# Softmax row sums from chunks added on Pool and split in two fp16 halves, in a fused attention and SwiGLU kernel

## Chip, cores, metric

One core of one Trainium2 chip. The metric is device microseconds of one execution; a quoted time is the median of three to seven executions, with the lowest and highest in brackets. "Clock" is the mean TensorE clock that the profile says was granted, as a share of full speed. Engines are named as in the profile: PE is TensorE, ACT is ScalarE, DVE is VectorE, POOL is GpSimd. SBUF and PSUM are the two kinds of memory that the kernel takes its tiles from: its matmuls write to tiles in PSUM (the pools with `space=PSUM`), and all other tiles lie in SBUF.

## The reference

Attention over 8 batches x 12 heads of 448 tokens with head size 64, then a gated feed-forward layer (FFN) over all 3584 tokens:

```python
scores = (q @ k.T) / sqrt(64);  attn = softmax(scores);  o = attn @ v     # per head
x = o.transpose(0, 2, 1, 3).reshape(3584, 768)
g = x @ w_gate                                  # 768 -> 1536
out = (g * sigmoid(g) * (x @ w_val)) @ w_out    # 1536 -> 768
```

Inputs and output are fp32. The kernel computes in fp16 with fp32 accumulation.

## The kernel before

Heads are worked in 48 *pairs*; two pairs (an even `p` and `p + 1`) make a *quad*, whose four heads go to four 32-column tiles of TensorE (form `112*32` in the profile; sixteen such matmuls of 0.355 us each, four a tile, take 0.76 us together). The program is one loop over pairs. A pass is called a *slot*; it computes the scores and exp of its own pair in two halves, and in between the row sums and PV (attn times v) of an earlier quad, and pieces of the FFN (gate `gp`, value `vp` and output `op` steps). The FFN pieces fill TensorE, so that it hardly has to wait for exp (2.2 us in all in the profile before).

`E[pr]` holds exp of the scores of a pair, transposed: keys on partitions, in 4 chunks of 112, and for each of the two heads 448 queries. The sum over keys is a matmul with a matrix of ones, 4 chunks x 4 heads = 16 matmuls a quad:

```python
def sums(p0):
    acc = ps_f.tile([128, 512], FP32, tag="f")
    for c in range(NC):                       # 4 chunks
        for j in range(4):                    # 4 heads of the quad
            nc.tensor.matmul(
                acc[ts(j, 32), 0:S], lhsT=ones[:],
                rhs=E[p0 + j // 2][:, c, j % 2, :],
                start=(c == 0), stop=(c == NC - 1),
            )
    ...
```

The loop, cut to what the change touches. Pool's queue takes, in this order: the copies of `prep` (order q and k for the transposing transfer), the loads of q and k, and in every third slot a load of v:

```python
for pr in range(END):
    ...
    qk_half(pr, 0)                              # scores, exp, chunks 0 and 1
    prep(pr + 3)                                # Pool: two copies
    if not odd: load_qk16(pr + LA)              # Pool issues two loads
    if (pr + 2) % GP == GP - 1: load_v(...)     # Pool issues a load of v
    if not odd: deferred.extend(recips(pr - 2, sums(pr - 2)))
    work = odd and pr > FIRST + 1
    if work: scaled(pr - 3, 0, pv(pr - 3, 0))   # PV, first half of the quad
    carry = ffn_run(...)                        # FFN steps; DVE's deferred work in between
    qk_half(pr, 1)                              # chunks 2 and 3
    if work: scaled(pr - 3, 1, pv(pr - 3, 1))   # PV, second half
    carry = ffn_run(...)
```

Each engine runs its own queue in program order (in slot 31 of the changed kernel, shown below, Pool's adds stand behind a load that waits 2.98 us). [...] The rest of the kernel is unchanged but for a scratch tile.

The softmax here doesn't subtract the row's maximum and nothing guards it: scores larger than these inputs give would overflow.

## Time and profile before

| | before |
|---|---|
| time, us (three executions; with a fourth, 463.63) | 463.38 (462.26 to 464.27) |
| span of the profiled execution, us | 460.2 |
| TensorE busy / idle in that span, us | 452.3 / 7.9 |
| TensorE clock | 1.00 |
| Pool busy, us | 104.2 |

Idle is span minus busy. TensorE is all but always at work, and 7.9 us of idle time is mostly the start and the end of the run. For such a kernel there is one question to a change: what does it take from TensorE's work, and what does it add to TensorE's waits?

### The profile page before, as it was taken

The numbers are of one execution on the slowest core, as the hardware profiler recorded it, in microseconds if no ns is written. First come the engines' busy times: TensorE is split into PE (matmuls) and PEld (weight loads), VectorE is DVE, ScalarE is ACT, GpSimd is POOL, SyncE is SP. The second block draws the span as 40 slices with busy tenths as digits, with TensorE's granted clock in tenths as the row PEclk, the third lists the DMA queues.
The fourth block names the chain that finished last, engine by engine and source line by source line (L and its number), as shares of the span: only waits on it lengthen the run. The fifth ranks groups of instructions, "written<-read, shape, count | busy, mean of one in ns | idle before, by whom it ended". The sixth has DMA issues, their size and how long they took to land.

```text
span 460.2 us, 14133 instructions
## 1 busy us (share of the span) xinstructions
PE 452.3 (98%) x6367; PEld 227.8 (49%) x6367; DVE 236.8 (51%) x371; ACT 243.0 (53%) x353; POOL 104.2 (23%) x164
## 2 busy tenths in 40 slices
PE   8899999999999999999999999999999999999996
PEld 3344444444455555444455555544445556554454
DVE  2765663666764554564654554636555546334310
ACT  7986666656664555454646555455555562222222
POOL 8455606334150132303123040210200000000000
PEclk9999999999999999999999999999999999999999
DMA  9999999995793484662758393903603111100123
GB/s 133 195 200 201 192 180 183 223 154 80 90 113 57 78 126 49 114 102 31 118 58 119 67 131 74 142 6 76 98 10 56 37 37 36 36 11 25 36 68 103
DMA packets 82045, 44.23 MB, mean 96 GB/s; under 512 B 36673, under 2 KB 78529, under 8 KB 81985
## 3 DMA queue, kind: packets, MB, share of 16 engines
q0 software_dynamic: 42368, 23.37, 39.2%
q1 hardware_dynamic: 39520, 19.92, 23.8%
q8 instruction: 49, 0.80, 0.7%
q14 instruction: 12, 0.09, 0.1%
q10 hardware_dynamic: 96, 0.05, 0.0%
HBM read 47.19 MB, written 11.01 MB: 126 GB/s over the span
## 4 chain that ended last, share of the span: by engine, by line
PE 95%; ACT 3%; DMA 1%; DVE 0%; issue 0%; SPq 0%; ACTq 0%
PE gp L264 15%; PE op L261 14%; PE vp L264 13%; PE vp L261 11%; PE op L264 10%; PE s L196 10%; PE gp L261 9%; PE acc L212 9%; PE acc L234 4%; ACT E L203 2%; DMA rk<-in_k_dram 1%; PE tp L184 1%; PE wp L103 0%; PE tp L167 0%; DVE qkT L175 0%
## 5 line engine op out<-in xcount | busy, mean ns | idle before, releaser
L203 ACT ACTIVATE E<-s 112x896 f16<-112x896 f32 x192 | 164.6, 917 | 24.3 <-PE s L196 24.1
L280 ACT ACTIVATE sg<-gp 128x384 f32<-128x384 f32 (+1 forms) x96 | 52.3, 545 | 85.4 <-PE gp L264 54.7
L292 DVE SCALAR_TENSOR_TENSOR t<-sg,gp 128x384 f32<-128x384 f32 (+1 forms) x96 | 58.5, 610 | 64.3 <-ACT sg L280 64.2
L325 ACT ACTIVATE osb<-op 128x384 f32<-128x384 f32 (+1 forms) x57 | 27.7, 486 | 100.5 <-PE op L261 56.3
L264 PE MATMUL gp<-X,wg 128*32 128x512 f16 (+1 forms) x1416 | 78.1, 355 | 0.0
L249 DVE RECIPROCAL R<-ssb 128x112 f32<-128x112 f32 x92 | 73.1, 827 | 0.7
L295 DVE SCALAR_TENSOR_TENSOR hts<-t,vp 128x384 f16<-128x384 f32 (+1 forms) x96 | 59.6, 621 | 23.3 <-PE vp L264 7.9
L261 PE MATMUL op<-wo,hts 128*128 128x384 f16 (+1 forms) x408 | 68.6, 322 | 0.0
L264 PE MATMUL vp<-X,wv 128*32 128x512 f16 (+1 forms) x1224 | 66.9, 353 | 0.0
L226 DVE TENSOR_TENSOR X<-acc,R 128x448 f16<-128x448 f32 x48 | 29.7, 624 | 64.9 <-PE acc L212 63.1
L261 PE MATMUL vp<-X,wv 128*128 128x384 f16 (+1 forms) x270 | 58.4, 352 | 0.0
L196 PE MATMUL s<-qkT 64*128 64x448 f16 x384 | 54.8, 355 | 2.5 <-ACT E L203 2.2
L261 PEld LDWEIGHTS <-hts 128*128 128x128 f16 x408 | 38.9, 98 | 28.2 <-issue 3.0
L264 PEld LDWEIGHTS <-wg 128*32 128x32 f16 x1416 | 37.8, 97 | 29.6
L264 PE MATMUL op<-wo,hts 128*32 128x384 f16 x1104 | 48.9, 326 | 0.0
L261 PE MATMUL gp<-X,wg 128*128 128x384 f16 (+1 forms) x222 | 47.4, 350 | 0.0
L264 PEld LDWEIGHTS <-wv 128*32 128x32 f16 x1224 | 32.7, 97 | 25.5
L212 PE MATMUL acc<-E,vt 112*32 112x448 f16 x768 | 45.2, 355 | 0.0
L126 POOL DMA_DIRECT2D vt<-in_v_dram x16 | 12.3, 772 | 142.7 <-PE acc L212 141.7
L261 PEld LDWEIGHTS <-wv 128*128 128x128 f16 x270 | 25.3, 98 | 26.9 <-issue 4.8
L264 PEld LDWEIGHTS <-hts 128*32 128x32 f16 x1104 | 29.5, 97 | 16.3
L154 POOL COPY qk<-q 112x512 f16<-112x512 f16 x37 | 22.9, 620 | 63.9 <-DMA qkT<-qk 46.4
(38 smaller groups left out, 201.2 us busy)
## 6 DMA issues: line engine op xcount, KB each, us to landing
vt<-in_v_dram POOLq DMA_DIRECT2D x16, 336.0 KB, 5.2
q<-in_q_dram POOLq DMA_DIRECT2D x22, 224.0 KB, 5.9
k<-in_k_dram POOLq DMA_DIRECT2D x22, 224.0 KB, 6.7
out_dram<-osb SPq DMA_DIRECT2D x7, 336.0 KB, 3.1
wg<-in_moe_w_gate_dram POOLq DMA_DIRECT2D x8, 288.0 KB, 11.1
wv<-in_moe_w_val_dram POOLq DMA_DIRECT2D x8, 288.0 KB, 11.4
wo<-in_moe_w_out_dram POOLq DMA_DIRECT2D x2, 1152.0 KB, 21.6
out_dram<-osb SPq DMA_DIRECT2D x8, 288.0 KB, 2.9
```

Of the source, the lines that this page charges most:

```text
L154: nc.gpsimd.tensor_copy(dst, src)
L196: nc.tensor.matmul(s[:, hx, 0:S], lhsT=t[ts(hx, 64)].rearrange("p c q -> p (c q)")[:, c * P : c * P + 128], rhs=t[ts(hx, 64), NC:, :].rear ...
L203: nc.scalar.activation(E[pr][:, c], s[0:P, :, 0:S], AF.Exp, scale=sm_scale)
L212: nc.tensor.matmul(acc[ts(j, 32), 0:S], lhsT=v16[g][:, 2 * r + j % 2, c, :].rearrange("p (d t) -> p t d", t=2)[:, t], rhs=E[p0 + j // 2][: ...
L226: nc.vector.tensor_tensor(X[kk][:, hp + t, ts(bb, S)], acc[:, 0:S], R[p0][:], ALU.mult)
L249: lambda i=i: nc.vector.reciprocal(rt[:, ts(i, P)], ssb[:, ts(i, P)]) for i in range(4)
L261: nc.tensor.matmul(dst, lhsT=lhsT, rhs=rhs, start=start, stop=stop)
L264: nc.tensor.matmul(dst[ts(j, 32), :], lhsT=lhsT[:, ts(j, 32)], rhs=rhs, start=start, stop=stop)
L280: nc.scalar.activation(sg[:, 0:n], gp[:, 0:n], AF.Tanh, scale=0.5)
L292: nc.vector.scalar_tensor_tensor(t1[:, 0:n], sg[:, 0:n], 1.0, gp[:, 0:n], ALU.add, ALU.mult)
L295: nc.vector.scalar_tensor_tensor(hts[:, fb, 0:n], t1[:, 0:n], 0.5 * HS, vp[:, 0:n], ALU.mult, ALU.mult)
L325: nc.scalar.activation(osb[:, ds(m0, w)], op[:, 0:w], AF.Copy, scale=1.0 / HS)
```

## The change

The intent: move part of the row sums from the bound engine to idle ones. For every other quad from pair 12 on (quads starting at 12, 16, 20 ... 40, eight in all), Pool adds the four chunks of E in fp32. So that TensorE can sum the result over partitions in fp16 without losing its precision, ACT rounds a quarter of the sum to fp16 (the high half) and DVE computes the rest (the low half); TensorE then needs 2 x 4 matmuls with a matrix of fours in place of 4 x 4. To give Pool time, from quad 12 on every quad's row sum and PV come one slot later: the sum in slot p + 3, PV in slot p + 4. So the quad that starts at 28 has its sum in slot 31.

```diff
+    def presummed(pr):
+        return PS <= pr < NPAIR - 4 and pr // 2 % 2 == 0          # PS = 12
+    def presum_a(pr):
+        ts_ = [attp.tile([P, S], FP32, tag="tsum", bufs=3, name="tsum") for _ in range(2)]
+        tsum[pr] = ts_
+        for hx in range(2):
+            nc.gpsimd.tensor_tensor(ts_[hx][:], E[pr][:, 0, hx], E[pr][:, 1, hx], ALU.add)
+    def presum_b(pr):
+        for hx in range(2):
+            t = tsum[pr][hx]
+            for c in (2, 3):
+                nc.gpsimd.tensor_tensor(t[:], t[:], E[pr][:, c, hx], ALU.add)
+    def presum_hi(pr):
+        hl[pr] = attp.tile([P, 2, 2, S], FP16, tag="hl", bufs=2, name="hl")
+        for hx in range(2):
+            nc.scalar.activation(hl[pr][:, 0, hx], tsum[pr][hx][:], AF.Copy, scale=0.25)
+    def presum_lo(pr, hx):
+        nc.vector.scalar_tensor_tensor(
+            hl[pr][:, 1, hx], tsum[pr][hx][:], 0.25, hl[pr][:, 0, hx], ALU.mult, ALU.subtract)
     def sums(p0):
-        for c in range(NC):
+        pre = presummed(p0)
+        n = 2 if pre else NC
+        for c in range(n):
             ...
-                    lhsT=ones[:],
-                    rhs=E[p0 + j // 2][:, c, j % 2, :],
+                    lhsT=ones[:, int(pre)],                       # ones or fours
+                    rhs=src[:, c, j % 2, :],                      # src: hl or E
 [... in the loop ...]
-            elif not odd and pr >= 2:
+            elif not odd and 2 <= pr < PS + 2:
                 deferred.extend(recips(pr - 2, sums(pr - 2)))
+            elif odd and pr >= PS + 3 and pr - 3 < NPAIR:
+                pop_deferred(99)
+                deferred.extend(recips(pr - 3, sums(pr - 3)))
+            if presummed(pr - 1):
+                presum_b(pr - 1)
 [... PV of quad pr - 3 or, from slot 16 on, of quad pr - 4; FFN; second half of scores; PV ...]
+            if presummed(pr):
+                presum_a(pr)
+            if presummed(pr - 1):
+                presum_hi(pr - 1)
+                for hx in range(2):
+                    deferred.append(lambda p=pr - 1, hx=hx: presum_lo(p, hx))
```

Cut from the diff: for room, the raw q and k tiles have four buffers in place of five (`RB`) and small pairs share them, and DVE's `t1` is written into `sg`. What is left of DVE's deferred work (reciprocals, low halves) is now all issued ahead of PV.

More of the change, by code (lines that the diff above doesn't have):

```diff
@@ L21 @@
 LA = 6
-RB = 5
+RB = 4
+PS = 12
 FIRST = 6
@@ L77 @@
     ps_f = ctx.enter_context(tc.tile_pool(name="ps_f", bufs=3, space=PSUM))
-    ones = consts.tile([P, 32], FP16, name="ones")
-    warm = consts.tile([128, 512], FP16, name="warm")
+    ones = consts.tile([P, 2, 32], FP16, name="ones")
+    warm = ep.tile([128, 512], FP16, tag="E", name="warm")
     ident = consts.tile([P, P], FP16, name="ident")
@@ L93 @@
     raw = {}
+    pairbuf = []
+    tsum = {}
+    hl = {}
     v16 = {}
@@ L112, in load_qk16 @@
     def load_qk16(pr, n=2):
-        q16 = raws.tile([P, 4, NC, D], FP16, tag="rq", bufs=RB, name="q16")
-        k16 = raws.tile([P, 4, NC, D], FP16, tag="rk", bufs=RB, name="k16")
-        for dst, src in ((q16, q), (k16, k)):
+        h0 = 2 if pr == 2 else 0
+        if h0 == 0:
+            pairbuf.clear()
+            for tag in ("rq", "rk"):
+                pairbuf.append(raws.tile([P, 4, NC, D], FP16, tag=tag, bufs=RB, name=tag))
+        for dst, src in zip(pairbuf, (q, k)):
             flat = src.rearrange("b h s d -> (b h) s d")[2 * pr : 2 * pr + 2 * n]
-            nc.gpsimd.dma_start(dst[:, 0 : 2 * n], flat.rearrange("h (p c) d -> p h (c d)", c=NC))
+            nc.gpsimd.dma_start(
+                dst[:, h0 : h0 + 2 * n], flat.rearrange("h (p c) d -> p h (c d)", c=NC)
+            )
         for i in range(n):
-            raw[pr + i] = (q16[:, 2 * i : 2 * i + 2], k16[:, 2 * i : 2 * i + 2])
+            raw[pr + i] = tuple(x[:, h0 + 2 * i : h0 + 2 * i + 2] for x in pairbuf)
     def load_v(g, lo=0, hi=2 * GP):
@@ L228, in scaled @@
         )
+    def presummed(pr):
[16 more added lines that the diff above has]
+        nc.vector.scalar_tensor_tensor(
+            hl[pr][:, 1, hx], tsum[pr][hx][:], 0.25, hl[pr][:, 0, hx], ALU.mult, ALU.subtract
+        )
     def sums(p0):
         acc = ps_f.tile([128, 512], FP32, tag="f")
-        for c in range(NC):
+        pre = presummed(p0)
+        n = 2 if pre else NC
+        for c in range(n):
             for j in range(4):
+                src = hl[p0 + j // 2] if pre else E[p0 + j // 2]
                 nc.tensor.matmul(
                     acc[ts(j, 32), 0:S],
-                    lhsT=ones[:],
-                    rhs=E[p0 + j // 2][:, c, j % 2, :],
+                    lhsT=ones[:, int(pre)],
+                    rhs=src[:, c, j % 2, :],
                     start=(c == 0),
-                    stop=(c == NC - 1),
+                    stop=(c == n - 1),
                 )
@@ L290, in ffn1_steps @@
                 )
-            t1 = fp.tile([128, 512], FP32, tag="t1")
             nc.vector.scalar_tensor_tensor(
-                t1[:, 0:n], sg[:, 0:n], 1.0, gp[:, 0:n], ALU.add, ALU.mult
+                sg[:, 0:n], sg[:, 0:n], 1.0, gp[:, 0:n], ALU.add, ALU.mult
             )
             nc.vector.scalar_tensor_tensor(
-                hts[:, fb, 0:n], t1[:, 0:n], 0.5 * HS, vp[:, 0:n], ALU.mult, ALU.mult
+                hts[:, fb, 0:n], sg[:, 0:n], 0.5 * HS, vp[:, 0:n], ALU.mult, ALU.mult
             )
@@ L354 @@
         nc.vector.memset(warm[:], 0.0)
-        nc.vector.memset(ones[:], 1.0)
+        nc.vector.memset(ones[:, 0], 1.0)
+        nc.vector.memset(ones[:, 1], 4.0)
         load_qk16(1, 1)
@@ L428 @@
         carry = 0.0
-        DELAY = 2
-        END = NPAIR + 2
+        END = NPAIR + 3
         add_at = {FIRST: 0}
         for i in range(1, B - 1):
-            add_at[NHP * (i + 1) + DELAY] = i
+            add_at[NHP * (i + 1) + (2 if NHP * i + 4 < PS else 3)] = i
         for pr in range(END):
@@ L470 @@
                     scaled(pr - 3, t, halves[t])
-            work = odd and pr > FIRST + 1
+            if presummed(pr - 1):
+                presum_b(pr - 1)
+            quad = None
+            if odd and FIRST + 1 < pr < PS + 3:
+                quad = pr - 3
+            if not odd and pr >= PS + 4:
+                quad = pr - 4
+            work = quad is not None
             if work:
-                pop_deferred(4)
-                scaled(pr - 3, 0, pv(pr - 3, 0))
+                pop_deferred(99)
+                scaled(quad, 0, pv(quad, 0))
             if pr in add_at and pr != FIRST:
@@ L495 @@
             if work:
-                scaled(pr - 3, 1, pv(pr - 3, 1))
+                scaled(quad, 1, pv(quad, 1))
+            if presummed(pr):
[4 more added lines that the diff above has]
+                    deferred.append(lambda p=pr - 1, hx=hx: presum_lo(p, hx))
             tiled[0] = pr >= TILED and work
```

## The prediction

"No such instruction" is an add of two tensors on Pool, the one-input copy is Pool's, and the 544 and 577 ns are ACT's single activations of 128 x 448. The sum came to 463.4 - 3.0 + 11.2 + 4.3 = 475.9 us and stands as recorded, but one term under it is cut: how long an add of 448 on Pool takes. No trace had such an add yet; the 1.1 us in Pool's steps (2.3 for two adds, 4.5 for four, and so in the 11.2 and 4.3) were the author's assumption. Rivals B and C: the 0.7 and 1.3 us there are assumptions.

> **What bounds the kernel now.** I read the page from the top: busy shares, the chain that ended last, then the groups, then the timeline of one stretch in mid-run, and last what Pool waited for.
>
> ```profile
> PE 452.3 (98%) x6367; PEld 227.8 (49%) x6367; DVE 236.8 (51%) x371; ACT 243.0 (53%) x353; POOL 104.2 (23%) x164
> ...
> PE 95%; ACT 3%; DMA 1%; DVE 0%; issue 0%; SPq 0%; ACTq 0%
> PE gp L264 15%; PE op L261 14%; PE vp L264 13%; PE vp L261 11%; PE op L264 10%; PE s L196 10%; PE gp L261 9%; PE acc L212 9%; PE acc L234 4%; ACT E L203 2%; DMA rk<-in_k_dram 1%; PE tp L184 1%; PE wp L103 0%; PE tp L167 0%; DVE qkT L175 0%
> ```
>
> The reader is to see that TensorE is the bound and the only one: it is on 95% of the chain, no other engine is over 53% busy, and Pool is idle for 77% of the time. So a matmul that goes is time won, and a wait of TensorE that comes is time lost. The row sums (L234) are 4% of the chain; that is what the change aims at. The timeline shows one slot of a pair:
>
> ```profile
> 254.76 0.55 PE L196 MATMUL s<-qkT 64*128 64x448 f16 x4
> ...
> 255.24 0.94 PE L234 MATMUL acc<-E,ones 112*32 112x448 f16 x16
> 255.26 1.72 ACT L203 ACTIVATE E<-s 112x896 f16<-112x896 f32 x2
> ...
> 256.00 2.12 PE L264 MATMUL op<-wo,hts 128*32 128x384 f16 x48
> ```
>
> A bar's length has the tail of the last matmul in it; the distance between starts is what TensorE spends. The 16 matmuls of a row sum take 256.00 - 255.24 = 0.76 us, so four of them (one chunk of E for four heads) take 0.19 us. In the same way, from starts in this and a neighbouring stretch: the four score matmuls 0.48 us, a half of PV 0.76, a gate or value step 1.0 (384 tokens) or 1.3 (512 tokens), an output step 2.0. A slot of one pair is about 9 us, and TensorE has no hole in it.
>
> [...] a matmul of 448 columns lasts 355 ns, yet sixteen take 0.76 us. [...] The trace has no such instruction; its one-input copy of 512 elements lasts 620 ns. [...] the trace has 544 ns for its 448-element one from PSUM and 577 ns for that from SBUF.
>
> **The change, part by part.** Presummed are the quads that start at pairs 12, 16, 20 ... 40: eight. *Removed:* in each, the row sum falls from 16 to 8 matmuls. That is 64 matmuls, 16 groups of 0.19 us: 3.0 us, all on the bound. *Moved:* sums and PV go to slots of the other parity and one pair later. In the built order the changes of tile shape on TensorE go from 218 to 219, and 36 full matmuls become 144 tiled ones, which cost the same (six full 384-column value matmuls and 24 tiled ones both take 1.0 us): nothing. E lives one pair longer, but with five buffers the sixth pair's exp still finds its buffer freed by a PV that stands earlier: nothing. One buffer fewer for raw q and k, and t1 in place: nothing, both have slack. *Added:* ACT 32 copies of 448 at 0.55 = 18 us; DVE 32 two-input operations of 448 at about 0.61 (L292: 540 ns at 384, 679 at 512) = 20 us; Pool 96 adds. [...] By busy time all of this fits beside TensorE.
>
> It does not fit by order. For a quad p, the second pair's chain is: Pool adds (four, two of them dependent), ACT high half, DVE low half, row sum on TensorE in slot p+3. Each queue is in order, so I laid the order of the changed program over the durations of the trace.
>
> *Quads 16, 28 and 40.* In slots 18, 30 and 42 Pool first has to issue a load of v, and in the changed order this load waits for the PV of the same slot's second half (in the kernel before, that PV was a slot earlier); the four adds stand behind it. The trace has what such a load costs:
>
> ```profile
> 213.85 1.47 PE L264 MATMUL gp<-X,wg 128*32 128x512 f16 x24
> ...
> 214.32 0.77 POOL L126 DMA_DIRECT2D vt<-in_v_dram  x1 [20.29 <-PE acc L212]
> ```
>
> Counting from the start of TensorE's first group after PV: the load issues from 0.5 to 1.2 us, the first tile's adds end at 3.5, the second's at 5.8, ACT's second copy at 6.4, DVE's second low half at 7.1; the row sum can go on at 7.2. TensorE arrives there after two FFN steps, scores and one group: 1.3 + 1.3 + 0.5 + 0.2 = 3.2 us for quad 16, 1.0 + 2.0 + 0.5 + 0.2 = 3.6 for 28 and 40. Holes: 4.0 + 3.6 + 3.6 = 11.2 us.
>
> *Quad 12.* Slot 14 has no PV (the shift by a pair leaves it out), so it is short. One fp32 buffer too few (three for four tiles) makes pair 13's second first-add wait for DVE's low half of pair 12; behind it stand two copies (1.1 us), two issues of q and k (1.4) and the four adds (4.5). With zero at the end of slot 13's PV: low half at 2.3, first-add to 3.4, copies to 4.5, issues to 5.9, adds to 10.4, ACT to 11.0, DVE to 11.7. TensorE: output step 2.0, scores 0.5, gate 1.3, scores 0.5, value and gate 2.6, scores 0.5, a group: 7.5. Hole: 4.3 us.
>
> *Quads 20, 24, 32 and 36* do the same with a whole PV slot of 9 us and no waiting load; the sum for 20 leaves TensorE about half a microsecond behind its data: no hole.
>
> Sum: 463.4 - 3.0 + 11.2 + 4.3 = 475.9 us.
>
> **The rivals.** *A: the chain fits, and only the removed matmuls count:* 460.4 us. For it: engines are half idle, and the alternation of quads and the extra pair look like they were made to give Pool time. Against it: the waiting load and the short slot are in the order. *B: the holes are there, but Pool adds are faster.* A copy starts every 0.555 us; if an add of 448 takes 0.7 us, the load quads win 1.6 us each and quad 12 2.0: holes 2.4 + 2.0 + 2.0 + 2.3 = 8.7, time 469. [...] *C: Pool becomes slower still*[...]: 1.3 us an add makes the holes 19 and the time 480. *D: a general wait*, ACT blocked by a high-half copy so that exp and tanh come late in all eight quads. Against it: outside the four slots Pool ends about when ACT arrives.
>
> **Range and chances.** I believe in holes in those slots at about 3 to 2, and in the add's duration within a factor of 1.5. Sized as estimated this is 476, with B 469, without holes 460; I take 471 as the middle and 461 to 479 as the range. Slower by 2% starts at 472.6, between B and my sum: 0.4. Faster by 2% would need 454.1, more than three times what is removed: 0.02. Within 2%: 0.58.
>
> **What would show it.** Right: L272 (row sums) with 320 matmuls; TensorE holes in front of the row sums of slots 15, 19, 31 and 43 with DVE's low half or ACT's high half as releaser, of 2 to 4.5 us each, and none elsewhere; Pool's v loads in slots 18, 30 and 42 waiting for PV; adds at 1.0 to 1.2 us; other stretches 0.38 us shorter for each presummed quad. Wrong: a PE idle sum under 1 us in front of row sums (then A), adds under 0.7 us (then B), small holes spread over all presummed quads (then D), or DVE and Pool durations grown by half (then C).

## The result, and the profile after

| | before | after |
|---|---|---|
| time, us | 463.63 (462.26 to 464.27) | 488.47 (487.83 to 493.87) |
| ratio of the times, after over before | | 1.0565 (95%: 1.0486 to 1.0645) |
| profiled span, us | 460.2 | 487.2 |
| TensorE busy / idle, us | 452.3 / 7.9 | 461.6 / 25.6 |
| TensorE clock, profiled / other runs | 1.00 | 0.989 / 0.979 to 0.993 |
| Pool busy, us | 104.2 | 207.4 |

All ratios here are computed as the mean time of one kernel's fast runs over that of the other's in the same rounds, so a ratio is not quite that of the two medians. The time is outside the predicted range of 461 to 479; the kernel is 5.6% slower.

The page of the changed kernel: busy shares, TensorE's clock in 40 slices (9 is 90% or more), and the chain that ended last, by engine and by line (share of the span).

```profile
PE 461.6 (95%) x6411; PEld 233.4 (48%) x6411; DVE 257.8 (53%) x404; ACT 256.9 (53%) x385; POOL 207.4 (43%) x260
...
PEclk9999999799899999999999999999999999999999
...
PE 37%; POOL 3%; ACT 1%; DVE 1%; issue 0%; POOLq 0%; ACTq 0%; DVEq 0%
PE op L299 8%; PE gp L302 6%; PE vp L302 5%; PE vp L299 5%; PE op L302 4%; PE gp L299 4%; PE acc L222 2%; PE s L206 2%; POOL tsum L253 2%; PE acc L272 1%; DVE hl L261 1%; ACT hl L258 0%; ACT E L213 0%; ACT osb L362 0%; POOL tsum L247 0%
```

The chain is followed back through only 42% of the span here, so its shares are not to be set against those of before. What is new in it is `POOL tsum`, `DVE hl` and `ACT hl`: a chain that was TensorE from end to end now runs through Pool. TensorE's idle time has grown by 17.7 us. And its *busy* time has grown by 9.3 us, though 64 matmuls went. A reason stands in the row of the clock: of the slices of 12.2 us each, the eighth (85 to 97 us) and the eleventh (122 to 134 us) are below 0.9. Slower matmuls count as more busy time (a value step that counts 1.47 us at full clock counts 2.65 behind slot 19).

The new instructions, in the groups of the changed kernel (count, then busy us and mean ns, then the idle time of the engine before them and what ended it):

```profile
L253 POOL TENSOR_TENSOR tsum<-tsum,E 112x448 f32<-112x448 f32 x64 | 67.9, 1071 | 5.8 <-ACT E L213 3.2
L247 POOL TENSOR_TENSOR tsum<-E 112x448 f32<-112x448 f16 x32 | 34.9, 1102 | 73.9 <-ACT E L213 40.3 <-DVE hl L261 33.6
L261 DVE SCALAR_TENSOR_TENSOR hl<-tsum,hl 112x448 f16<-112x448 f32 x32 | 23.8, 758 | 21.9 <-ACT hl L258 21.8
```

The adds last what was predicted (1.1 us), ACT's copies a little more than that (0.58 for 0.55), and DVE's low halves clearly more (0.76 for 0.61).

The waits of the changed kernel (us in all, how many, the longest):

```profile
POOL tsum L247 <- DVE hl L261: 33.6, 7, 6.4
...
POOL vt L136 <- PE acc L222: 32.8, 4, 12.9
...
PE acc L272 <- ACT hl L258: 9.5, 7, 2.0
...
PE s L206 <- ACT E L213: 4.3, 8, 1.5
PE acc L272 <- DVE hl L261: 4.0, 7, 0.6
...
PE op L302 <- DVE sg L329: 2.3, 1, 2.3
```

The row sums (L272) wait 13.5 us for the two halves. A score step waits for exp, and one output step for DVE. Pool in its turn waits for DVE's low half in seven places (for a free `tsum` buffer), and for PV in the loads of v.

Here is one of the waits in full, in the timeline of the changed kernel: quad 28, whose row sum is in slot 31. Columns: start, length, engine and line, and in brackets how long the engine had been idle and what released it.

```profile
233.17 1.47 PE L302 MATMUL vp<-X,wv 128*32 128x512 f16 x24
233.64 0.77 POOL L136 DMA_DIRECT2D vt<-in_v_dram  x1 [2.98 <-PE acc L222]
234.42 4.53 POOL L253 TENSOR_TENSOR tsum<-tsum,E 112x448 f32<-112x448 f32 x4
...
237.01 0.59 PE L272 MATMUL acc<-hl,ones 112*32 112x448 f16 x3
...
238.99 0.58 ACT L258 ACTIVATE hl<-tsum 112x448 f16<-112x448 f32 x1 [1.79 <-POOL tsum L253]
...
239.61 0.37 PE L272 MATMUL acc<-hl,ones 112*32 112x448 f16 x4 [2.01 <-ACT hl L258]
...
240.59 0.35 PE L272 MATMUL acc<-hl,ones 112*32 112x448 f16 x1 [0.60 <-DVE hl L261]
```

Pool stood still for 2.98 us for PV, then issued the load, then added for 4.53 us; ACT and DVE split the last tile, and TensorE, at the sum since 237.01, issued its last matmul at 240.59. From PV's end (233.17) the data were ready after 7.4 us (predicted 7.2) and TensorE was there after 3.8 (predicted 3.6).

Pool's chain from there on is the predicted one almost to the tenth.

I measured the other waits in the same way: from the first to the last start of the eight matmuls of a sum, less 0.33 us, an estimate for seven unhindered starts (7 x 0.0475, from 0.76 us for 16; in the one sum that waits for nothing, in slot 35, they take 0.21, so each wait is good to 0.1 us or so). The 1.89 us in the scores of slot 14 are the profile's idle time. These come to more than the 17.7 us by which the profile's idle time has grown, because the profile counts the last matmul before a wait as busy to the end of its 0.35 us. In us, with what was predicted:

| quad (slot of its sum) | predicted | measured |
|---|---|---|
| 12 (15) | 4.3 | 1.89 waited in the scores of slot 14, 1.69 in slow steps ahead of the sum, 2.88 waited in the sum: 6.46 |
| 16 (19) | 4.0 | 3.89 |
| 28 (31), 40 (43) | 3.6 + 3.6 | 3.25 + 3.28 |
| 20, 24, 36 (23, 27, 39) | none | 0.82 + 1.55 + 1.55 |
| 32 (an output step in slot 34) | none | 2.30 |
| sum | 15.5 | 23.1 |
| steps behind the sums of slots 15 and 19, at a lower clock | none | 1.37 + 1.86 = 3.2 |

Two of these rows need a closer look, for the reason is not the predicted one. Pool's load of v for quad 16, and DVE's low halves and Pool's first-add for quad 24 (changed kernel):

```profile
122.41 0.77 POOL L136 DMA_DIRECT2D vt<-in_v_dram  x1 [0.17 <-issue]
...
189.02 1.16 DVE L261 SCALAR_TENSOR_TENSOR hl<-tsum,hl 112x448 f16<-112x448 f32 x2
...
189.79 1.29 POOL L247 TENSOR_TENSOR tsum<-E 112x448 f32<-112x448 f16 x1 [4.16 <-DVE hl L261]
```

Quad 16's load stood idle for only 0.17 us, and not for PV: Pool had come to it late, because its first-add before had waited 4.32 us for a buffer. For quad 24, the adds of the first pair had ended at 184.64, but ACT wrote the high halves from 186.43 to 187.48, and DVE began the low halves at 189.02, behind two multiplications of the FFN in its queue. Pool waited 4.16 us for the buffer that they free, and its last add ended at 198.11, after TensorE had come to the sum at 197.87.

The last row of the table comes from TensorE's timeline near slot 19. The sum ends at 129.34; behind it come a value and a gate step of 512 tokens, which take 1.3 and 1.4 us elsewhere. TensorE alone, changed kernel:

```profile
129.34 0.35 PE L272 MATMUL acc<-hl,ones 112*32 112x448 f16 x1 [0.61 <-DVE hl L261]
129.34 2.65 PE L302 MATMUL vp<-X,wv 128*32 128x512 f16 x24
131.44 2.53 PE L302 MATMUL gp<-X,wg 128*32 128x512 f16 x24
133.90 0.55 PE L206 MATMUL s<-qkT 64*128 64x448 f16 x4
```

The wait and the steps by windows (window, its length; busy us and count of PE, PEld, DVE, ACT, POOL; then the granted clock, the busy share of the DMA engines and GB/s):

```profile
126.43:129.84 3.41, 0.87 (x16) 0.45 (x19) 1.45 (x3) 2.10 (x4) 3.41 (x5) 1.00 1.14 152
129.84:133.25 3.41, 3.41 (x40) 1.96 (x36) 2.33 (x4) 0.57 (x1) 1.85 (x3) 0.50 0.76 113
```

The steps took 2.10 and 2.46 us, and TensorE was 100% busy, at half clock from 129.84 to 133.25. That is 1.86 us lost *after* the wait (4.56 less 2.70). Behind the sum of slot 15 the steps took 2.50 and 1.57, a loss of 1.37. The two steps behind the score wait of slot 14 were slow as well (2.30 and 2.09, 1.69 too much); these 1.69 stand with quad 12, because they lie ahead of its sum, where TensorE would otherwise have arrived earlier and waited longer. Behind the 3.3 us waits of slots 31 and 43 the steps stayed at 1.31 and 1.29: no loss there.

Why behind some waits and not behind others? The traces record when the clock was granted, and the record settles it for this case. The clock in it is either 1.00 or 0.50, and it changes only on a grid of 3.41 us that runs through the whole execution (in the changed kernel the record begins at 10.37 us, changes at 88.88, 92.29, 95.70, 99.12, 129.84 and 133.25 us, and ends just behind the span, 140 steps after its begin) and lies differently in each (counted from the start of the span its edges lie at whole steps plus 0.95 us in the kernel before, plus 0.13 in the changed kernel). The changed kernel has three stretches of half clock, from 88.88, 95.70 and 129.84 us; at half clock each costs up to half of 3.41, so 5.1 us together (an estimate), and 1.69 + 1.37 + 1.86 = 4.9 were measured. For each stretch of the grid one can estimate the share in which matmuls stream (from their starts in the traces, with 0.16 to 0.22 us for one, by its size: six in a row take 0.97 to 0.99 us at 384 columns and 1.30 at 512). In all thirteen profiled executions there are 1726 stretches at full clock. After each of the 18 with a share of 0.36 or less the clock was half; after each of the others, all at 0.40 or more, it stayed full. The three here had 0.32, 0.33 and 0.20. The wait of slot 31 fell across two stretches, which kept 0.45 and 0.61. So it is not the length of a wait alone that decides, but also how it lies on the grid. By the mean clocks, the four executions of the changed kernel had about 3, 6, 2 and 3 stretches at half clock (an estimate), and the one with 6 is the slow one of 493.87 us.

Do these parts make the whole? The best base is the profile of the order shift alone (experiment 1, span 463.2): 463.2 - 3.0 for the removed matmuls + 23.1 + 3.2 = 486.5, and the span was 487.2. The remaining 0.7 us stay unassigned. The agreement is in part luck: that profile is the slowest of its kernel's four executions, and with the span of the other three (461.8 to 461.9) 2 us would remain.

### The profile page after: what moved, and what is told of

It reads as the page before. It is cut to its first block, busy times and chain, and to the rows that moved or that the text cites. A ratio compares the mean times of both kernels' runs of the same rounds, so it can differ in the third digit from the quotient of the medians.

```text
span 487.2 us, 14444 instructions
## 1 busy us (share of the span) xinstructions
PE 461.6 (95%) x6411; PEld 233.4 (48%) x6411; DVE 257.8 (53%) x404; ACT 256.9 (53%) x385; POOL 207.4 (43%) x260
## 5 line engine op out<-in xcount | busy, mean ns | idle before, releaser
L213 ACT ACTIVATE E<-s 112x896 f16<-112x896 f32 x192 | 164.3, 917 | 12.4 <-PE s L206 12.2
L329 DVE SCALAR_TENSOR_TENSOR sg<-sg,gp 128x384 f32<-128x384 f32 (+1 forms) x96 | 58.4, 608 | 59.7 <-ACT sg L318 59.6
L302 PE MATMUL gp<-X,wg 128*32 128x512 f16 (+1 forms) x1440 | 82.2, 358 | 0.0
L302 PE MATMUL vp<-X,wv 128*32 128x512 f16 (+1 forms) x1296 | 74.1, 360 | 0.0
L332 DVE SCALAR_TENSOR_TENSOR hts<-sg,vp 128x384 f16<-128x384 f32 (+1 forms) x96 | 59.6, 621 | 24.0 <-PE vp L302 8.5
L253 POOL TENSOR_TENSOR tsum<-tsum,E 112x448 f32<-112x448 f32 x64 | 67.9, 1071 | 5.8 <-ACT E L213 3.2
L247 POOL TENSOR_TENSOR tsum<-E 112x448 f32<-112x448 f16 x32 | 34.9, 1102 | 73.9 <-ACT E L213 40.3
L302 PEld LDWEIGHTS <-wg 128*32 128x32 f16 x1440 | 41.5, 98 | 32.1 <-issue 5.2
L299 PE MATMUL vp<-X,wv 128*128 128x512 f16 (+1 forms) x252 | 55.8, 358 | 0.0
L302 PE MATMUL op<-wo,hts 128*32 128x384 f16 x1152 | 51.2, 326 | 2.3 <-DVE sg L329 2.3
L302 PEld LDWEIGHTS <-wv 128*32 128x32 f16 x1296 | 37.0, 98 | 28.0 <-issue 3.3
```

What stands on the lines that cost most here:

```text
L213: nc.scalar.activation(E[pr][:, c], s[0:P, :, 0:S], AF.Exp, scale=sm_scale)
L247: nc.gpsimd.tensor_tensor(ts_[hx][:], E[pr][:, 0, hx], E[pr][:, 1, hx], ALU.add)
L253: nc.gpsimd.tensor_tensor(t[:], t[:], E[pr][:, c, hx], ALU.add)
L299: nc.tensor.matmul(dst, lhsT=lhsT, rhs=rhs, start=start, stop=stop)
L302: nc.tensor.matmul(dst[ts(j, 32), :], lhsT=lhsT[:, ts(j, 32)], rhs=rhs, start=start, stop=stop)
L329: nc.vector.scalar_tensor_tensor(sg[:, 0:n], sg[:, 0:n], 1.0, gp[:, 0:n], ALU.add, ALU.mult)
```

## The experiments

Each is an edit of the changed kernel, was correct against the reference, and was timed against the kernel before on the same chip. Eleven were run. Differences under 2% of the time, as in 4, 5, 7, 8 and 10, are read from the intervals of their ratios.

**1. The shift alone.** Is some of the loss in the later row sums, the lost `q`/`k` buffers, or the tile shapes, and not in the presums?

```diff
 def presummed(pr):
-    return PS <= pr < NPAIR - 4 and pr // 2 % 2 == 0
+    return False
```

> No quad is presummed; the sums and the PV one pair later, E's longer life and the smaller buffers for raw q and k stay. Theory (only the new Pool, ACT, DVE chain in front of the row sums costs): within 1 us of the kernel before, 462.5 to 464.6, no TensorE wait in front of a row sum, clock 1.00. Rival (the shift or the lost buffers cost by themselves): 467 us or more.

463.67 us (463.57 to 465.02) beside 463.68; ratio 1.0007 (0.9975 to 1.0039). The shift, the buffers and `t1` cost nothing that shows: by the interval, 1.8 us at most. The loss is in the presums.

**2. The v load behind the adds.** The load that waits for PV is issued at the end of the slot, so that Pool's adds stand ahead of it.

```diff
-    load_v((pr + 2) // GP + 1)         # ahead of presum_b
 ...
     if work: scaled(quad, 1, pv(quad, 1))
+    if late_v: load_v((pr + 2) // GP + 1)
     if presummed(pr): presum_a(pr)
```

> The changed kernel with Pool's load of v behind the adds of its slot, not ahead of them. Theory (the load that waits for the same slot's PV holds up the adds of quads 16, 28, 40): the waits in front of the row sums of slots 19, 31 and 43, now 3.9, 3.3 and 3.3 us, fall to what quads 24 and 36 show (about 1.6) or less, the other quads' stay, so 480 to 484 us. Rival (ACT and DVE stages[...] make the waits): they stay over 3 us and the time stays at 487 to 490.

482.82 us (481.19 to 484.06); ratio 1.0411 (1.0373 to 1.0449). The waits of slots 31 and 43 are gone: their eight matmuls take 0.6 us or less where they took 3.6. The order of Pool's queue, and nothing else, made those two. In slot 19 the wait stayed, against what I expected, and changed its releaser. The timeline of this run there:

```profile
125.52 2.30 DVE L261 SCALAR_TENSOR_TENSOR hl<-tsum,hl 112x448 f16<-112x448 f32 x1 [1.53 <-ACT hl L258]
...
125.61 0.62 POOL L164 COPY qk<-rq 112x512 f16<-112x512 f16 x1
...
127.28 1.01 POOL L164 COPY qk<-rk 112x512 f16<-112x512 f16 x1
127.87 0.35 PE L272 MATMUL acc<-hl,ones 112*32 112x448 f16 x1 [1.96 <-DVE hl L261]
```

The low half of DVE took 2.30 us; the shortest one of this run took 0.56. It began 0.09 us ahead of the first of four Pool copies in a row and lasted until the last of them was under way, and that copy in turn took 1.01 us for the usual 0.6. So in this run a two-input operation of DVE and copies of Pool were slow where they ran at the same time; the trace doesn't show why.

**3. A fourth fp32 buffer.** With three `tsum` buffers, Pool's second first-add of a quad's second pair waits for DVE. A fourth takes that wait away. Room came from computing the reciprocals in place.

```diff
-    ... tag="tsum", bufs=3, ...
+    ... tag="tsum", bufs=4, ...
-    ssb = attp.tile([128, S], FP32, tag="ssb", bufs=1)
-    nc.vector.tensor_copy(ssb[:], acc[:, 0:S])
+    nc.vector.tensor_copy(rt[:], acc[:, 0:S])          # reciprocals in place in R
```

> The changed kernel with four fp32 sum buffers for the four sums of a quad, not three (the room comes from making the reciprocals in place). Theory (the fourth sum waits for DVE's low half of the first pair, and the rest of Pool's queue behind it is late): the waits in front of the row sums of slots 15, 23, 27 and 39 and the one at quad 32 go under 0.3 us, those of slots 19, 31 and 43 stay at over 3 us; 474 to 481 us. Rival (Pool is simply too slow for six adds a pair): all waits stay within 0.5 us and the time within 3 us of the changed kernel.

484.8 us (482.53 to 486.9); ratio 1.0455 (1.0406 to 1.0504); profiled span 482.1. The waits that I had not predicted are gone: the sums of quads 20, 24, 32 and 36 take 0.6, 0.4, 0.4 and 0.4 us, and the output step of slot 34 doesn't wait. So the fourth buffer is what those four quads lacked; the low halves are no faster than before (0.85 us on average). The sums of slots 19, 31 and 43 still take 3.6 to 4.2 us, as expected. That of slot 15 takes 3.4, which I had expected to shrink, and the time stayed above my expectation of 474 to 481. Part of that is the clock: here the same waits of slots 31 and 43 were each followed by a stretch at half clock, and the two steps behind them took 4.1 and 4.2 us for 2.6, so 3.2 us more.

**4. Both.** Edits 2 and 3.

> Both mends together. Theory (the two orders on Pool's queue are the whole loss): no wait over 0.5 us in front of any row sum, clock at 0.997 or more, and the 3.0 us of removed matmuls show: 459.5 to 463 us. Rival (Pool throughput[...]): waits of 1 us and more remain in most presummed quads, 467 us or more.

472.03 us (471.99 to 473.32); ratio 1.018 (1.0145 to 1.0215). That saves more than the two edits apart (16.4 for 5.7 + 3.7), because each alone leaves the wait in slot 19. But I had expected 459.5 to 463, all of it. What remains is mostly quad 12 (slot 19 still waits 1.0 us, the other sums about 0.3 or nothing). TensorE's timeline of this run:

```profile
91.25 0.37 PE L272 MATMUL acc<-hl,ones 112*32 112x448 f16 x2
92.82 0.35 PE L272 MATMUL acc<-hl,ones 112*32 112x448 f16 x1 [1.20 <-ACT hl L258]
95.18 0.57 PE L272 MATMUL acc<-hl,ones 112*32 112x448 f16 x4 [2.01 <-ACT hl L258]
96.16 0.53 PE L272 MATMUL acc<-hl,ones 112*32 112x448 f16 x1 [0.41 <-DVE hl L261]
```

The sum takes 4.9 us, and the score step of slot 14 waits 1.3 more (5.9 us of waits in all, with 0.33 taken off as above). With no buffer missing, Pool simply has too much to do there: from its two first-adds at 85.08 to the end of its four later adds at 94.52 it is never idle, 9.4 us in a row: two adds of 1.2, two copies, two issues of 0.7 and four adds of 1.13. TensorE's part of this, slot 14 without PV, is too short to cover it. From the score wait of slot 14 to the end of the sum it is 9.2 us in this run, and 9.2 in the changed kernel, with slow steps in between there and none here: Pool's chain sets that time, whatever TensorE does. The two steps behind the sum took 2.53 and 3.05 us at the lower clock.

**5. Both, from quad 16 on.** `PS = 16` in the kernel of experiment 4: seven quads, and the short slot lies before the first of them.

> The two mends, and presumming starts with quad 16: seven quads. Theory (what is left of the loss is quad 12, whose six adds a pair do not fit into the short slots 12 to 14, and the low clock after its waits): no wait over 1 us, clock 0.998 or more, 463.7 - 7 x 0.38 = 461.0, so 460.3 to 462.5 us. Rival (the first presummed quad is always late, or Pool lacks throughput everywhere): quad 16 shows waits over 3 us and the time stays over 466 us.

464.55 us (463.84 to 465.23); ratio 1.0026 (1.0006 to 1.0047), clock 1.00. A miss: I had expected 460.3 to 462.5. The 24 us of loss are gone but for one wait, and so is the gain. The wait is in slot 19 again, 2.0 us, and again DVE's low halves lie beside Pool's copies. In this run's timeline:

```profile
116.30 3.10 DVE L261 SCALAR_TENSOR_TENSOR hl<-tsum,hl 112x448 f16<-112x448 f32 x2 [0.15 <-ACT hl L258]
...
119.45 0.35 PE L272 MATMUL acc<-hl,ones 112*32 112x448 f16 x1 [0.60 <-DVE hl L261]
```

Two low halves took 3.10 us (the longer 2.16; the shortest of the run 0.62). With 7 x 0.38 = 2.7 us removed and 2.0 waited, 0.7 us of gain should be left and isn't: about 1.8 us of this kernel's time I can't place. The three sums in slots 23, 31 and 43 that take 0.6 us for 0.4 are a part of it.

**6. Is it the waiting that slows the clock?** Useless matmuls (12 in slot 15, 18 in slots 19, 31 and 43, 384 columns, 0.17 us each) stand ahead of the row sums, where TensorE would wait anyway. They change no result.

```diff
+    if pr in (15, 19, 31, 43):
+        wp = ps_f.tile([128, 512], FP32, tag="f", name="wp")
+        for _ in range(12 if pr == 15 else 18):
+            nc.tensor.matmul(wp[:, 0:OH], lhsT=wo[0][:, 0, 0:128], rhs=wo[0][:, 1], start=True, stop=True)
     deferred.extend(recips(pr - 3, sums(pr - 3)))
```

> The changed kernel with matmuls of no use ahead of the row sums of slots 15 (12 of 0.16 us), 19, 31 and 43 (18 each), inside the waits. Theory (the idle TensorE is what lowers its clock, and the low clock costs about 5 us on top of the waits): the waits after the dummies are 1 us or less in 19, 31 and 43, value and gate steps behind slot 19 take 1.3 us and not 2.1 to 2.5, clock 0.993 or more, and the time falls although TensorE got more work: 483 to 486.5 us. Rival (the clock falls for another reason): the steps behind slot 19 stay over 2 us, clock 0.989 or less, the time is 488 us or more.

The same steps of TensorE behind slot 19 in this run:

```profile
128.96 0.35 PE L272 MATMUL acc<-hl,ones 112*32 112x448 f16 x1 [0.60 <-DVE hl L261]
128.96 1.64 PE L302 MATMUL vp<-X,wv 128*32 128x512 f16 x24
130.27 1.63 PE L302 MATMUL gp<-X,wg 128*32 128x512 f16 x24
```

1.31 and 1.57 us where the changed kernel took 2.10 and 2.46: with the wait filled, the clock held. From the score step's end to the end of these steps it is 7.1 us in place of 8.8. So far as expected. But the time is 487.82 us (486.99 to 488.52), ratio 1.0528 (1.0506 to 1.055), and not the 483 to 486.5 that I had expected. Around slot 15 half a microsecond was lost and not won: Pool's chain sets the time up to the sum (9.2 us again), the twelve matmuls left 2.5 us of waiting in it, and the steps behind were slow all the same (1.94 and 2.62). And the 2.3 us wait of quad 32, which I hadn't filled, was followed by an output step of 2.81 us in place of 2.06, which had kept its clock before. The grid accounts for it: the wait of quad 32 fell into one stretch here (share 0.36) and across two in the changed kernel (0.73 and 0.55). What the run shows: the clock stays up behind a filled wait (slot 19). What it doesn't show is how much is to be won so.

**7. The same quads without the split.** Pool adds chunks 0 and 1, and chunks 2 and 3, straight to fp16, for both heads in one instruction of 896 elements; TensorE sums the two halves, again with 8 matmuls a quad. No ACT stage, no DVE stage, no fp32 buffer; Pool's load of v stays where the changed kernel has it. In 7 to 10 the reciprocals are computed in place, as in 3, and `hl` has four buffers for two. The diff is shortened: its first line is in words, and `as 896` stands for joining the two heads.

```diff
-    (six fp32 adds of 448 a pair in presum_a and presum_b, high half on ACT, low half on DVE)
+    def presum_half(pr, i):              # i = 0 in presum_a, 1 in presum_b
+        nc.gpsimd.tensor_tensor(hl[pr][:, i] as 896, E[pr][:, 2 * i], E[pr][:, 2 * i + 1], ALU.add)
```

> The same eight quads, the same matmuls saved and the v load where the change has it, but Pool adds chunks in pairs (0+1 and 2+3) to fp16, both heads in one instruction: two adds of 896 a pair and no ACT or DVE stage. Theory (the long chain of Pool, ACT and DVE is what makes the waits): the adds end 3.4 us after PV in the load slots, before TensorE comes, so waits under 0.5 us everywhere and 463.7 - 3.0 = 460.7, 459.5 to 462.5 us. Rival (Pool's waiting load alone makes them): 2 us and more of wait at slots 19, 31 and 43, 466 us or more.

460.65 us (460.38 to 461.98); ratio 0.9948 (0.9927 to 0.9969). The removed matmuls' worth, 2.8 us of the 3.0, is there at last. Pool's adds in the groups of this run:

```profile
L248 POOL TENSOR_TENSOR hl<-E 112x896 f16<-112x896 f16 x32 | 60.4, 1890 | 56.4 <-ACT E L213 56.3
```

Pool's work for a pair falls from six adds of 1.08 (6.5 us) to two of 1.89 (3.8 us), and the two stages behind it (0.6 + 0.8 us) are gone. No row sum waits for Pool, although the load of v still waits for PV (73.1 us in eight places). The waiting load is a loss only where the chain behind it is long. The price is precision: each half is rounded to fp16 once.

**8. All quads.** The same with all 18 quads from 12 on, and the load of v behind.

```diff
-    return PS <= pr < NPAIR - 4 and pr // 2 % 2 == 0
+    return PS <= pr < NPAIR
```

> The fp16 pair adds for all 18 quads from 12 on, with the v load behind the adds. Theory: Pool has about 4.2 us of adds beside 2.1 us of its old work in a slot of 7 to 9 us, so it keeps up: 18 x 0.38 = 6.8 us less than the kernel before, 456 to 458.5 us. Rival (Pool cannot keep up in consecutive quads): waits in front of the sums and 460 us or more.

458.23 us (457.27 to 459.12); ratio 0.989 (0.9865 to 0.9916). 18 quads x 0.38 = 6.8 us removed, 5.2 won.

**9. The third add on DVE.** As 8, but the two halves of a quad are added once more, by DVE with two SBUF inputs, so that TensorE needs 4 matmuls a quad.

```diff
+    def presum_c(pr):
+        nc.vector.tensor_tensor(hl[pr][:, 0], hl[pr][:, 0], hl[pr][:, 1], ALU.add)
-    n = 2 if pre else NC
+    n = 1 if pre else NC
```

> As the fp16 kernel for 18 quads, and DVE adds the two halves, so that one matmul a head is left. By removed matmuls alone: 458.2 - 18 x 0.19 = 454.8 us, 453.5 to 456.5, if DVE's two-input add[...] stays off the path (DVE is half idle and the sum is needed a slot later). Rival[...]: DVE's add takes well over its 0.6 us, the FFN multiplications behind it in DVE's queue come late and TensorE waits for a PSUM buffer: 458 us or more.

496.61 us (493.06 to 499.02); ratio 1.0706 (1.0644 to 1.0768): slower than everything else, with the fewest matmuls of all. All occurrences of DVE's add in this run (shortest, median and longest, in ns):

```profile
L260 DVE TENSOR_TENSOR hl<-hl x36: 563/1376/7340, 82.5 to 409.6; 112x896 f16<-112x896 f16 x36
```

The longest one, in the timeline of this run:

```profile
230.19 1.90 POOL L248 TENSOR_TENSOR hl<-E 112x896 f16<-112x896 f16 x1
...
231.09 7.34 DVE L260 TENSOR_TENSOR hl<-hl 112x896 f16<-112x896 f16 x1
...
233.15 3.69 POOL L248 TENSOR_TENSOR hl<-E 112x896 f16<-112x896 f16 x2
...
237.35 0.60 POOL L164 COPY qk<-rk 112x512 f16<-112x512 f16 x1
237.91 0.73 POOL L125 DMA_DIRECT2D rq<-in_q_dram  x1
238.49 0.56 PE L279 MATMUL acc<-hl,ones 112*32 112x448 f16 x2 [5.37 <-DVE hl L260]
```

DVE began its add while Pool was in one of its own, and was not done through two copies, two adds and two more copies of Pool. It ended at 238.43, half a microsecond after Pool's last copy, when Pool had come to an instruction that only issues a transfer; half a microsecond is what the shortest add of this run takes (0.56). TensorE waited 5.37 us for it, 17.7 us for such adds in all, and 8.0 us more at two gate steps for the multiplications behind them in DVE's queue. So DVE's two-input add, too, is slow beside Pool's adds and copies, here without the split and without missing buffers, and it costs more than any other thing that I tried. Experiment 10, with the same add on Pool, has none of these waits. The clock fell to 0.967, with nine stretches at half clock.

**10. The third add on Pool.** As 9, with the add on Pool, from quad 20 on (14 quads with 4 matmuls, 4 with 8).

```diff
+    if pr >= 20:                          # in presum_b, behind presum_half(pr, 1)
+        nc.gpsimd.tensor_tensor(hl[pr][:, 0], hl[pr][:, 0], hl[pr][:, 1], ALU.add)
-    n = 2 if pre else NC
+    n = (1 if p0 >= 20 else 2) if pre else NC
```

> The same third add, but on Pool, for the 14 quads from 20 on. Pool has 3 x 1.9 + 2.1 = 7.8 us of work in a slot of about 9 us. If it keeps up: 458.2 - 14 x 0.19 = 455.5, 454.5 to 457 us. If it falls behind (copies for the transposes late, sums late): 459 us or more.

455.99 us (454.75 to 456.14); ratio 0.983 (0.981 to 0.9851), faster than both kernels (1.7% less than the kernel before, clear of noise). From its page:

```profile
PE 445.4 (98%) x6275; PEld 224.3 (49%) x6275; DVE 234.8 (52%) x372; ACT 241.0 (53%) x353; POOL 290.1 (64%) x264
```

Pool is far busier than in the changed kernel (290 us for 207) and TensorE waits for nothing new but 0.5 us. Pool's busy share was never the trouble. 9.5 us of matmuls are gone (200 x 0.0475) for 7.4 won; where the rest went, here and in 8, I didn't follow up.

**11. The changed kernel from quad 16 on.** `PS = 16` alone, to size what quad 12 costs.

> The changed kernel with presumming from quad 16 on, seven quads, nothing else touched. Theory (quad 12, in the short slots, costs 5.2 us of waits and about 1.4 us of low clock behind them): 488.5 - 6.6 + 0.4 = 482, in 480 to 484 us, with no wait at 87 and 93 us of the run and quads 28 and 40 as they were. Rival (whichever quad comes first takes these waits): quad 16 shows 5 us or more and the time stays above 486 us.

480.96 us (479.62 to 481.13); ratio 1.0376 (1.0356 to 1.0396). Quad 12 costs 7.5 us. The table above has for it 6.46 + 1.37 behind its sum - 0.38 of removed matmuls = 7.45. So a part of the account is confirmed by a run that takes it out.

## Why the prediction was wrong

The reading of the bound, the removed work, and the cause of the loss were right: a chain Pool, ACT, DVE in program order that arrives later than TensorE. Point by point:

- *Removed 3.0 us:* right. Experiment 7 has them (2.8).
- *Moved: nothing:* right (experiment 1).
- *Adds of 1.1 us:* right (1.07 and 1.10, the shortest of both 1.03), so rival B fell. The 1.1 itself was an assumption. By element that is 2.4 to 2.5 ns, and the fp16 add of 896 in experiment 7 (1.89 us) has 2.1.
- *Holes of 4.0 + 3.6 + 3.6 in slots 19, 31 and 43, because the load of v waits for PV:* right within 0.4 us, and experiment 2 shows the cause for two of them. In slot 19 the size was luck. Either of two causes is enough there, the load or the wait for a buffer with a slow low half of DVE behind it (2.30 us in experiment 2), and in the changed kernel it was the buffer: the load stood idle for 0.17 us only.
- *Quad 12, 4.3 us:* the place is right, the size too small (6.5), and one link not needed. (The prediction's own steps of TensorE add up to 7.6 us and not 7.5, so its hole is 4.1 or 4.2.) Without the missing buffer, on which I had built the step, there are still 5.9 us of waits (experiment 4): the slot is too short for Pool's own work. A part of the wait moved ahead to the scores of slot 14, where ACT's high half, waiting for Pool, stands in front of exp. That is the mechanism of rival D, in one slot.
- **"Quads 20, 24, 32 and 36 ... no hole": this step failed.** TensorE waited 6.2 us there. I had counted a whole PV slot and half a microsecond of lead. What I had wrong is Pool's wait for the third buffer: 33.6 us in seven places, 4.2 us for quad 24, because the high and low halves of the first pair come late in the queues of ACT and DVE (4.4 us from the end of the adds to the start of DVE for quad 24). Experiment 3, which takes away the buffer wait, removes all four. That the low halves are slow (0.76 us on average for the 0.61 that I had) is not the reason: for quad 24 the two took 1.16 us, and in experiment 3 they are slower still. So two-input operations of DVE that are slow beside Pool's work, for which I had no term, are not needed here; they show in slot 19 (2.30 us in experiment 2, 2.16 in experiment 5) and in experiment 9 (up to 7.34).
- **No term for TensorE's clock: this was missing from the sum.** The trace before, from which the sum was made, shows a clock of 1.00 throughout. With waits of TensorE the clock was half after stretches of 3.41 us of the grid with matmuls in up to 36% of them, so a stretch need not be idle for it, and the four executions of the changed kernel had mean clocks from 0.979 to 0.993. Behind the sums it cost 3.2 us, and 1.7 more are in quad 12's 6.5.
- *The hedge.* The written sum was 475.9; I recorded 471, because I believed in the holes "at about 3 to 2". The four predicted holes were all there, three at their sizes and one larger. The list of half-believed reasons for less was balanced by none for more.

From 471.0 to 488.5 there are 17.5 us: the hedge 4.9, the four quads 6.2, the clock 3.2, quad 12 2.2, less 0.8 by which quads 16, 28 and 40 waited less than predicted, and 1.8 that I can't assign.

What was measured of DVE beside Pool: the two-input low half went from 0.56 to 2.30 us beside Pool's copies (experiment 2), and DVE's two-input add from 0.56 to 7.34 beside copies and adds (experiment 9). Why, no run of this case shows.

What stays open: 1.8 us of experiment 5, the 1.6 and 2.1 us by which experiments 8 and 10 won less than was removed, and the 0.7 to 2 us of the changed kernel that no part of the account holds.

## What to carry to other kernels

When work moves from the bound engine to an idle one, lay out the chain of queues up to the moment when the bound engine needs the result, with everything that each queue has ahead of it: busy shares say nothing about that (Pool at 43% cost 25 us, Pool at 64% won 7). A wait that is put on TensorE can cost more than its length: in the changed kernel 1.37 to 1.86 us of clock behind each of three stretches of 3.41 us in which matmuls streamed for 20 to 33%. Give an estimate of waits a term for that, and don't shade a sum that was worked out step by step toward the hoped-for end. Prefer one longer stage on one engine to three short ones on three, and keep DVE's operations on two SBUF tensors out of the time of Pool's copies and adds (here up to 2.30 and 7.34 us for 0.56).
